# Weight norms moved to TensorE, weight scaling moved to ScalarE, and a first layer that works on column pairs

## The chip, the cores and the metric

The kernel runs on one core of one Trainium2 chip. The metric is device time in microseconds (us) of one execution; the time of before is the median of three runs.

## The reference, cut to what matters

The inputs are float64 or float32 arrays; q, k and v have batch 2, 8 heads, 768 positions, head size 64. The two feed-forward layers have 1536 tokens, model size 512 and hidden size 2048.

```python
q_assign = argmax(q_n . c_n);  k_assign = argmax(k_n . c_n)      # 16 clusters, per head
scores = where(q_assign == k_assign, q @ k.T / 8, -1e9)
x = softmax(scores) @ v                                          # to [1536, 512]
h = x @ w_in;   x = (h * sigmoid(h)) @ w_out                     # "first weights", first layer
h = x @ w2_in;  out = (max(h, 0) + alpha * min(h, 0)) @ w2_out   # second weights, second layer
```

Precision near that of float32 is wanted. So each operand of a matmul is scaled by a power of two and split in a high and a low half in 16 bits, and each product is made of three matmuls (high by high, high by low, low by high).

## The kernel before, in words

**Units.** Attention is cut into 12 query tiles of 128 rows by 8 heads, 96 units. For a unit, `maxima` makes the scores and VectorE takes the row maxima (L514); every second unit `to_rows` (L518) turns the maxima of a pair of units into extra rows of an operand by four small VectorE instructions (L525 to L530), a matmul (L535) and a copy (L537); `weights` makes the scores again, transposed, takes the exponential on ScalarE (L560), makes the high half on ScalarE (L566) and the low half on VectorE (L567); `values` multiplies by v in 20 matmuls (L582 to L592). `x_done` normalises four heads at a time and, after a tile's second half, transposes the tile by a DMA into the operand of the first layer.

**Weights.** Each of the four weight matrices arrives as eight pieces of 1 MB, of float64, so 128 x 1024 numbers of two 32-bit words. `to_f32` (L650) turns a piece into float32: ScalarE converts the low word (L656), the high word is scaled by GpSimd (L664, mode "p") or by ScalarE (L660, mode "a"), and VectorE joins them in two instructions (L667, L670). `sum_sq` (L696) then squares the piece on ScalarE and adds up along the row, a matmul with a matrix of ones (`all_sum`, L222) adds up over the rows, and `pow2_scale` (L171 to L178) makes a power of two of that. `split` (L675) makes the halves: in mode "d" the high one on GpSimd (L677), in mode "a" the same on ScalarE (L682), and in both the low one on VectorE (L678, L683); in mode "b" two instructions are ScalarE's (L687, L688) and one GpSimd's (L689). The strings `SPLIT` and `EXP_ON` (L38, L39) choose the modes piece by piece; their first two entries are the first layer's w_in and w_out. For the first layer's w_in a piece is converted and, one task later, scaled and split; all of w_out is converted first, and its eight splits are run together in `w1_finish` (L789), which the loop calls at step 16 of the first chunk (L1114). GpSimd also makes low halves of k and v (L359, L382).

**First layer.** `layer1` (L899) handles seven chunks of tiles, two of one tile (128 columns) and five of two tiles (256 columns). Each of 16 blocks f of 128 hidden units has 12 matmuls into a PSUM bank (L929), then tanh on ScalarE (L935), a product on VectorE that also frees the bank (L936), the high half on ScalarE (L939) and the low half on VectorE (L940). Then four output blocks take 48 matmuls each (L960) and one ScalarE instruction (L967). The banks come from a pool of two, kind "w".

**Order.** The main loop (L1100 to L1130) runs attention to unit 17, and then gives each chunk 32 steps; after each it advances attention, so that by the end of chunk c the units reach `UNITS_BY_CHUNK[c]` (L24). After a unit, `run_bg` runs as many weight tasks as `W_TASKS` says. The batch-1 keys and values are prepared between units 36 and 56. When the last unit is out, `w2_start` begins the conversion of the second weights, whose buffers lie where attention's keys were; meanwhile the remaining first-layer steps fill TensorE. The build's scheduler then fixes the order of the instructions in each engine's queue; it may place later steps before earlier ones where nothing depends on them. Then `layer2` runs three groups of 512 columns (L1032, L1041 to L1046, L1063).

## Time and profile of before

| what | value |
|---|---|
| median of three runs | 892.24 us (890.08 to 893.33) |
| profiled execution, its own time | 892.16 us |
| its span, first to last instruction | 890.3 us |
| mean granted TensorE clock | 0.986 |
| TensorE matmul busy | 771.0 us (87% of the span) |
| VectorE busy | 622.7 us (70%) |
| ScalarE busy | 481.4 us (54%) |
| GpSimd busy | 151.5 us (17%) |

The profile is of one execution. PE is TensorE's matmuls, PEld its weight loads, DVE is VectorE, ACT is ScalarE, POOL is GpSimd and SP the queue that issues DMAs; L12 is line 12 of the kernel. Ends of matmuls are modelled, so a busy PE is not PE at its peak. Shares over the whole span mix stages with different limits, so the tables below are by stretch, in us from the start of the span. The time outside the span is 892.16 - 890.3 = 1.9 us.

### The profile page before, as it was taken

The page shows a single profiled execution, that of the slowest core. Times are in us where ns is not written, and L with a number is a line of the kernel's source. Part 1 is how long each engine was busy: PE and PEld are TensorE (multiplying, and loading weights), DVE is VectorE, ACT ScalarE, POOL GpSimd, SP SyncE. Part 2 cuts the span into 40 slices and gives each one's busy share as a digit, 9 for nine tenths or more (in the row PEclk, how much of TensorE's full clock was granted, in tenths as well). Part 3 has the DMA queues.
Part 4 walks back from the last instruction along what each step waited for, and adds up shares of the span by engine and source line. Part 5 has one row for each costly group of instructions (what it writes and reads, how often), then busy time and mean ns, then how long its engine had stood idle before and what let it go on. Part 6 is the DMA issues. An engine that isn't in the chain of part 4 may idle for free.

```text
span 890.3 us, 19036 instructions
## 1 busy us (share of the span) xinstructions
PE 771.0 (87%) x8068; PEld 564.9 (63%) x8068; DVE 622.7 (70%) x1379; ACT 481.4 (54%) x817; POOL 151.5 (17%) x142
## 2 busy tenths in 40 slices
PE   2365379889999999999999968969989999999998
PEld 1254268778888788888888856758534444444443
DVE  8999978997987856965876778586896048305700
ACT  7745658846878736755764686787723013102200
POOL 5744200150023210000000003441650000000000
PEclk9999999979999999999999999999999999999999
DMA  8946720322244321120103045444000000000000
GB/s 276 291 114 216 204 64 15 61 59 33 61 83 98 67 62 25 38 48 14 25 14 37 14 147 170 163 149 173 18 1 1 36 13 0 13 25 13 1 23 25
DMA packets 91077, 64.28 MB, mean 72 GB/s; under 512 B 66800, under 2 KB 77040, under 8 KB 90864
## 3 DMA queue, kind: packets, MB, share of 16 engines
q1 hardware_dynamic: 90992, 63.07, 26.6%
q8 instruction: 63, 1.03, 0.5%
q14 instruction: 22, 0.18, 0.1%
HBM read 44.08 MB, written 3.15 MB: 53 GB/s over the span
## 4 chain that ended last, share of the span: by engine, by line
PE 47%; DVE 8%; ACT 4%; DMA 3%; issue 1%; POOL 1%; ACTq 0%; DVEq 0%; POOLq 0%
PE w L1063 9%; PE w L1032 7%; PE w L960 7%; PE w L929 6%; PE m L1063 5%; PE m L1032 4%; PE s L557 2%; PE s L558 2%; DVE arena L1046 2%; DMA arena<-in_moe_w_out_dram 2%; PE s L506 2%; PE s L510 2%; DMA arena<-in_moe_w_in_dram 1%; DVE arena L667 1%; DVE arena L670 1%
## 5 line engine op out<-in xcount | busy, mean ns | idle before, releaser
L929 PE MATMUL w<-arena 128*128 128x256 f16 (+1 forms) x1212 | 129.1, 256 | 6.5 <-DVE arena L936 6.3
L960 PE MATMUL w<-arena 128*128 128x256 f16 (+1 forms) x1200 | 127.3, 259 | 6.5 <-DVE arena L678 4.0
L929 PEld LDWEIGHTS <-arena 128*128 128x128 f16 x1344 | 115.0, 98 | 26.0 <-issue 12.5
L960 PEld LDWEIGHTS <-arena 128*128 128x128 f16 x1344 | 116.3, 100 | 20.0 <-DVE arena L678 4.4
L560 ACT ACTIVATE arena<-s,stat 128x768 f32<-128x768 f32 x96 | 86.2, 898 | 69.9 <-PE s L558 62.8
L514 DVE TENSOR_REDUCE stat<-s 128x1 f32<-128x768 f32 x96 | 91.5, 954 | 40.2 <-PE s L510 39.4
L1032 PEld LDWEIGHTS <-arena 128*128 128x128 f16 x576 | 56.7, 99 | 73.0 <-issue 7.2
L567 DVE TENSOR_TENSOR arena<-arena 128x768 f16<-128x768 f32 x96 | 94.1, 980 | 8.7 <-ACT arena L566 8.3
L1063 PEld LDWEIGHTS <-arena 128*128 128x128 f16 x576 | 56.2, 98 | 68.1
L1032 PE MATMUL w<-arena 128*128 128x512 f16 x384 | 87.8, 385 | 4.0 <-DVE arena L1042 4.0
L664 POOL TENSOR_SCALAR arena<-arena 128x1024 f32<-128x1024 f32 x28 | 40.6, 1454 | 284.5 <-DMA arena<-in_moe_w_in_dram 224.2
L557 PE MATMUL s<-arena 120*128 120x128 f16 x576 | 83.0, 229 | 4.4 <-ACT arena L537 4.3
L1063 PE MATMUL w<-arena 128*128 128x512 f16 x384 | 83.9, 379 | 0.0
L1045 ACT ACTIVATE arena<-arena,stat 128x512 f16<-128x512 f32 x48 | 34.6, 721 | 90.8 <-DVE arena L1042 88.9
L558 PE MATMUL s<-arena 128*128 128x128 f16 x576 | 83.1, 230 | 0.0
L566 ACT ACTIVATE arena<-arena 128x768 f16<-128x768 f32 x96 | 80.3, 836 | 1.1
L588 PE MATMUL x<-arena 128*128 128x65 f16 x576 | 68.7, 198 | 11.2 <-DVE arena L567 11.2
L582 PE MATMUL x<-arena 128*128 128x65 f16 x576 | 74.3, 198 | 4.4 <-ACT arena L566 4.0
L506 PE MATMUL s<-arena 80*128 80x384 f16 x192 | 67.1, 350 | 11.7 <-DMA arena<-arena 6.7
L585 PE MATMUL x<-arena 128*128 128x64 f16 x576 | 74.6, 199 | 0.0
L510 PE MATMUL s<-arena 128*128 128x384 f16 x192 | 67.5, 352 | 0.0
L588 PEld LDWEIGHTS <-arena 128*128 128x128 f16 x576 | 56.4, 102 | 14.5 <-DVE arena L567 12.5
(163 smaller groups left out, 1506.6 us busy)
## 6 DMA issues: line engine op xcount, KB each, us to landing
arena<-in_moe_w_in_dram SPq DMA_DIRECT2D x16, 1024.0 KB, 6.2
arena<-in_moe_w_out_dram SPq DMA_DIRECT2D x16, 1024.0 KB, 4.9
arena<-in_k_dram SPq DMA_DIRECT2D x8, 384.0 KB, 4.4
arena<-in_q_dram SPq DMA_DIRECT2D x6, 512.0 KB, 4.6
arena<-in_v_dram SPq DMA_DIRECT2D x8, 384.0 KB, 6.0
out_dram<-arena SPq DMA_DIRECT2D x12, 256.0 KB, 2.0
arena<-in_moe_alpha_dram SPq DMA_DIRECT2D x1, 1024.0 KB, 4.7
arena<-arena SPq DMA_TRANSPOSE x53, 3.6
```

Of the source, the lines that this page charges most:

```text
L506: nc.tensor.matmul(out=out, lhsT=qt2[0:D + C], rhs=kt2[0:D + C, j * th:(j + 1) * th], start=True, stop=False,)
L510: nc.tensor.matmul(out=out, lhsT=qt1, rhs=kt1[:, j * th:(j + 1) * th], start=False, stop=True,)
L514: nc.vector.tensor_reduce(out=un_cols[:, c:c + 1], in_=sc[:, :, :S // 2], axis=AX.XY, op=ALU.max, negate=True)
L557: nc.tensor.matmul(out=out, lhsT=kt2[0:k, t], rhs=qt2[0:k], start=True, stop=False)
L558: nc.tensor.matmul(out=out, lhsT=kt1[:, t], rhs=qt1, start=False, stop=True)
L560: nc.scalar.activation(out=view(o, F32, 2, S // 2), in_=sc[:, :, :S // 2], func=ACTF.Exp, scale=d[:, pr:pr + 1],)
L567: nc.vector.tensor_tensor(out=pt[:, 1], in0=p, in1=pt[:, 0], op=ALU.subtract)
L588: nc.tensor.matmul(out=out, lhsT=pt[:, T + t], rhs=vt[:, t, 0:D + 1], start=False, stop=False)
L929: nc.tensor.matmul(out=hp, lhsT=wi[:, a, kd, f % 2 * 128:f % 2 * 128 + 128], rhs=mov(bb, kd), start=(i == 0), stop=(i == 3 * KD - 1),)
L960: nc.tensor.matmul(out=acc, lhsT=wo[:, a, f % 2, dt * 128:(dt + 1) * 128], rhs=g[:, f, bb], start=(i == 0), stop=(i == 3 * KF - 1),)
L1032: nc.tensor.matmul(out=hp, lhsT=in_piece(o_a + 24 * KB, f // 2)[:, a, kd, f % 2 * 128:][:, :128], rhs=x[bb][:, kd], start=(i == 0), stop=( ...
L1063: nc.tensor.matmul(out=acc, lhsT=g[:, f, a, t * 128:(t + 1) * 128], rhs=out_piece(o_w, f // 2)[:, bb, f % 2], start=(i == 0), stop=(i == 3 ...
```

## The change

The high word of each piece of the first weights is scaled by ScalarE, not GpSimd; their high halves are made by ScalarE, all sixteen of them (14 were GpSimd's, two of mode "b"). Their sums of squares come from `gram`: eight matmuls of 128 columns multiply the upper 16 bits of a piece's float32 numbers by themselves into one bank, and one VectorE instruction multiplies the diagonal out and adds it up along the row. `layer1` takes two blocks into one bank and does tanh, product, high and low half on both at once; the number of steps stays. `to_rows` has three VectorE instructions, not four, with a constant in another row of the keys' operand, for which `prep_k_a` has two more GpSimd memsets. The chunk targets move. The second weights keep their modes.

```diff
--- before.py
+++ after.py
@@ -21,7 +21,7 @@
 
 
 UNITS_FIRST = 17
-UNITS_BY_CHUNK = (32, 53, 64, 69, 98, 98, 98)
+UNITS_BY_CHUNK = (30, 42, 62, 82, 98, 98, 98)
 W_TASKS = (
     2, 2, 2, 2, 1, 1, 1, 1, 2, 2, 2, 2, 2, 2, 2, 2,
     1, 1, 1, 1, 2, 2, 3, 2, 1, 1, 1, 1, 1, 1, 1, 1, 1, 1, 1, 1, 2, 2, 2, 2,
@@ -35,8 +35,8 @@
 
 K_SCALE_ON = ("aaaa", "pppa")
 V_SCALE_ON = ("papa", "appp")
-SPLIT = ("dddddddd", "dddbdddb", "dbdbdbdb", "dccdcbbc")
-EXP_ON = ("pppppppp", "pppppppp", "appppapp", "papapppp")
+SPLIT = ("aaaaaaaa", "aaaaaaaa", "dbdbdbdb", "dccdcbbc")
+EXP_ON = ("aaaaaaaa", "aaaaaaaa", "appppapp", "papapppp")
 
 
 
@@ -119,7 +119,7 @@
     o_g = region(16 * KB)
     o_x2 = region(24 * KB)
     o_xt = region(12 * KB)
-    o_tmp = region(3 * KB)
+    o_tmp = region(4 * KB)
     o_a = region(0)
     o_kt1 = region(12 * KB)
     o_kt2 = region(12 * KB)
@@ -137,6 +137,7 @@
     o_id = region(256)
     o_ml = region(256)
     o_sel = region(288)
+    o_junk = region(256)
     o_one = region(1024)
     total = pos[0]
     arena = arena_p.tile([128, total // 4], F32, name="arena")
@@ -347,6 +348,8 @@
         for i in range(2):
             r = MROW + 2 * (2 * pr + i)
             nc.gpsimd.memset(w2[:, i * T:(i + 1) * T, r:r + 2], MASK)
+            r = FROW + 2 * pr + i
+            nc.gpsimd.memset(w2[:, i * T:(i + 1) * T, r:r + 1], -MASK)
         if b == 0 and pr == 0:
             s = kv_state.pop("s")
             nc.scalar.activation(out=w1[:, :, D:2 * D], in_=kr, func=ACTF.Copy, scale=s)
@@ -403,9 +406,9 @@
                     stop=(t == T - 1),
                 )
         hi, lo = sv[:, 0, 4 * w:4 * w + 4], sv[:, 1, 4 * w:4 * w + 4]
-        nc.scalar.activation(out=hi, in_=ps, func=ACTF.Copy, scale=2.0 ** -5)
+        nc.scalar.activation(out=hi, in_=ps, func=ACTF.Copy, scale=1.0 / MASK)
         nc.vector.scalar_tensor_tensor(
-            out=lo, in0=ps, scalar=2.0 ** -5, in1=hi, op0=ALU.mult, op1=ALU.subtract
+            out=lo, in0=ps, scalar=1.0 / MASK, in1=hi, op0=ALU.mult, op1=ALU.subtract
         )
 
     def v_scales(b):
@@ -521,14 +524,15 @@
         n, h = divmod(u, H)
         pr = h // 2
         nm = un_cols[:, 2 * (u // 2 % 3):2 * (u // 2 % 3) + 2]
-        c = scr(2)
-        nc.vector.tensor_scalar(c, nm, 2.0 ** 29, 1.0 / MASK, op0=ALU.min, op1=ALU.mult)
         r = MROW + 4 * pr
         parts = ml[:, r:r + 4].rearrange("p (a b) -> p a b", b=2)
-        nc.vector.tensor_copy(out=parts[:, :, 0], in_=c)
-        nc.vector.tensor_tensor(out=parts[:, :, 1], in0=c, in1=parts[:, :, 0], op=ALU.subtract)
+        nc.vector.tensor_scalar(parts[:, :, 0], nm, 1.0 / MASK, None, op0=ALU.mult)
+        nc.vector.scalar_tensor_tensor(
+            out=parts[:, :, 1], in0=nm, scalar=1.0 / MASK, in1=parts[:, :, 0],
+            op0=ALU.mult, op1=ALU.subtract,
+        )
         nc.vector.tensor_scalar(
-            ml[:, FROW + 2 * pr:FROW + 2 * pr + 2], nm, 2.0 ** 29, 2.0 ** 5,
+            ml[:, FROW + 2 * pr:FROW + 2 * pr + 2], nm, 2.0 ** 29, MASK,
             op0=ALU.is_ge, op1=ALU.mult,
         )
         ps = psum("m", 128)
@@ -695,6 +699,18 @@
     def sum_sq(t, junk, ss):
         nc.scalar.activation(out=junk, in_=t, func=ACTF.Square, accum_out=ss)
 
+    def gram(tb, ss):
+
+
+        ps = psum("w", 128)
+        for i in range(PC // 128):
+            c = tb[:, i * 128:(i + 1) * 128]
+            nc.tensor.matmul(out=ps, lhsT=c, rhs=c, start=(i == 0), stop=(i == PC // 128 - 1))
+        nc.vector.scalar_tensor_tensor(
+            out=view(o_junk, BF16, 128), in0=ps, scalar=1.02, in1=ident, op0=ALU.mult,
+            op1=ALU.mult, accum_out=ss,
+        )
+
     def in_tasks(w, raws, o_dst, kind, modes, mp):
 
         m = Weight()
@@ -712,7 +728,10 @@
         def conv(j):
             t, junk = (raw(j)[:, :, i].bitcast(F32) for i in (1, 0))
             to_f32(raw(j), t, mp[j])
-            sum_sq(t, junk, ss[:, j:j + 1])
+            if w2:
+                sum_sq(t, junk, ss[:, j:j + 1])
+            else:
+                gram(view(raws[j % len(raws)], BF16, PC, 4)[:, :, 3], ss[:, j:j + 1])
 
         def scale(j):
             if not w2:
@@ -757,7 +776,10 @@
                     assert ("k", 0, o // 6) in did
             t = view(o_ts[j], F32, PC)
             to_f32(raw(j), t, mp[j])
-            sum_sq(t, raw(j)[:, :, 0].bitcast(F32), ss[:, j:j + 1])
+            if w2:
+                sum_sq(t, raw(j)[:, :, 0].bitcast(F32), ss[:, j:j + 1])
+            else:
+                gram(view(o_ts[j], BF16, PC, 2)[:, :, 1], ss[:, j:j + 1])
             load(j + len(raws))
 
         def scale():
@@ -914,32 +936,34 @@
         first = t0 % T == 0
         if c and first:
             nc.vector.tensor_scalar(dh, w1["in"].inv, x_inv[b], 0.5, op0=ALU.mult, op1=ALU.mult)
-        for f in range(KF):
-            j = f // 2
+        for j in range(NPC):
             wi = in_piece(o_w, j)
-            if c == 0 and f % 2 == 0:
+            if c == 0:
                 nc.vector.tensor_scalar(
                     dh[:, j:j + 1], w1["in"].inv[:, j:j + 1], x_inv[b], 0.5,
                     op0=ALU.mult, op1=ALU.mult,
                 )
-            hp = psum("l", n)
-            i = 0
-            for kd in range(KD):
-                for a, bb in ((0, 0), (0, 1), (1, 0)):
-                    nc.tensor.matmul(
-                        out=hp, lhsT=wi[:, a, kd, f % 2 * 128:f % 2 * 128 + 128], rhs=mov(bb, kd),
-                        start=(i == 0), stop=(i == 3 * KD - 1),
-                    )
-                    i += 1
-            th = view(o_tmp + KB * ring("t1", 3), F32, n)
-            nc.scalar.activation(out=th, in_=hp, func=ACTF.Tanh, scale=dh[:, f // 2:f // 2 + 1])
+            hp = psum("l", 2, n)
+            for r in range(2):
+                i = 0
+                for kd in range(KD):
+                    for a, bb in ((0, 0), (0, 1), (1, 0)):
+                        nc.tensor.matmul(
+                            out=hp[:, r], lhsT=wi[:, a, kd, r * 128:r * 128 + 128], rhs=mov(bb, kd),
+                            start=(i == 0), stop=(i == 3 * KD - 1),
+                        )
+                        i += 1
+                if r == 0:
+                    yield
+            th = view(o_tmp + 2 * KB * ring("t1", 2), F32, 2, n)
+            nc.scalar.activation(out=th, in_=hp, func=ACTF.Tanh, scale=dh[:, j:j + 1])
             nc.vector.scalar_tensor_tensor(
                 out=th, in0=th, scalar=1.0, in1=hp, op0=ALU.add, op1=ALU.mult
             )
-            nc.scalar.activation(out=g[:, f, 0], in_=th, func=ACTF.Copy, scale=2.0 ** -16)
+            hi, lo = g[:, 2 * j:2 * j + 2, 0], g[:, 2 * j:2 * j + 2, 1]
+            nc.scalar.activation(out=hi, in_=th, func=ACTF.Copy, scale=2.0 ** -16)
             nc.vector.scalar_tensor_tensor(
-                out=g[:, f, 1], in0=th, scalar=2.0 ** -16, in1=g[:, f, 0],
-                op0=ALU.mult, op1=ALU.subtract,
+                out=lo, in0=th, scalar=2.0 ** -16, in1=hi, op0=ALU.mult, op1=ALU.subtract,
             )
             yield
         g1_done.add(c)
```

## Rows read from the trace of the kernel before

**Rows 1.** Stretches: busy us (x) of PE, PEld, DVE, ACT, POOL; clock; DMA.

```profile
40.00:133.00 93.00, 50.62 (x562) 40.57 (x563) 86.60 (x162) 51.69 (x72) 33.05 (x21) 0.98 0.56 157
...
176.00:194.00 18.00, 13.81 (x164) 12.15 (x162) 18.00 (x15) 7.85 (x11) 14.32 (x12) 0.72 0.13 33
...
194.00:320.00 126.00, 116.68 (x1889) 103.62 (x1887) 101.91 (x304) 92.85 (x178) 19.30 (x20) 1.00 0.38 76
...
320.00:525.00 205.00, 203.48 (x2752) 179.55 (x2751) 145.92 (x397) 125.23 (x219) 1.32 (x1) 1.00 0.15 28
...
525.00:665.00 140.00, 113.12 (x889) 84.04 (x887) 111.67 (x164) 95.54 (x159) 56.96 (x32) 0.96 0.37 125
```

**Rows 2.** Timeline, 91 to 94 us: start, us, engine, instruction.

```profile
91.18 1.13 POOL L664 TENSOR_SCALAR arena<-arena 128x1024 f32<-128x1024 f32 x1 [1.13 <-DMA arena<-in_moe_w_out_dram]
...
91.43 1.95 DVE L667 SCALAR_TENSOR_TENSOR arena<-arena 128x1024 int32<-128x1024 int32 x1
```

**Rows 3.** DVE groups, 40 to 133 us; last, L667 over the span, min/median/max.

```profile
L667 DVE SCALAR_TENSOR_TENSOR arena<-arena 128x1024 int32<-128x1024 int32 x14 | 22.5, 1610 | 2.6 <-POOL arena L664 1.5 <-ACT arena L537 1.1
...
L670 DVE SCALAR_TENSOR_TENSOR arena<-arena 128x1024 int32<-128x1024 int32 x14 | 18.9, 1348 | 0.0
...
L667 DVE SCALAR_TENSOR_TENSOR arena<-arena x32: 1207/1226/2608, 14.7 to 627.2; 128x1024 int32<-128x1024 int32 x32
```

**Rows 4.** POOL groups, 40 to 133 us.

```profile
L664 POOL TENSOR_SCALAR arena<-arena 128x1024 f32<-128x1024 f32 x13 | 18.5, 1433 | 29.1 <-DMA arena<-in_moe_w_out_dram 27.3 <-ACT arena L696 1.8
...
L677 POOL TENSOR_SCALAR arena<-arena,stat 128x1024 f16<-128x1024 f32 x6 | 12.1, 2022 | 13.4 <-DVE stat L178 10.9 <-DVE stat L175 2.4
```

**Rows 5.** Two PE matmuls at 107 us; PE group of fp32 matmuls, whole span.

```profile
107.29 0.31 PE L557 MATMUL s<-arena 120*128 120x128 f16 x1
...
107.40 0.31 PE L558 MATMUL s<-arena 128*128 128x128 f16 x1
...
L222 PE MATMUL m<-arena 128*128 128x128 f32 x4 | 1.3, 409 | 4.7 <-DVE arena L407 4.7
```

**Rows 6.** ACT groups of the span, 1024 wide.

```profile
L696 ACT ACTIVATE arena<-arena 128x1024 f32<-128x1024 f32 x32 | 36.9, 1152 | 30.5 <-DVE arena L670 27.8 <-DVE stat L175 2.7
...
L660 ACT ACTIVATE arena<-arena 128x1024 f32<-128x1024 f32 x4 | 4.5, 1116 | 0.0
...
L696 ACT ACTIVATION_READ_ACCUMULATOR arena<-arena 128x1 f32 x32 | 6.2, 195 | 0.0
```

**Rows 7.** DVE and POOL groups, 173 to 194 us; then DVE timeline there.

```profile
L678 DVE SCALAR_TENSOR_TENSOR arena<-arena,stat 128x1024 f16<-128x1024 f32 x6 | 12.9, 2188 | 0.0
...
L677 POOL TENSOR_SCALAR arena<-arena,stat 128x1024 f16<-128x1024 f32 x6 | 9.3, 1571 | 58.2 <-DVE stat L950 58.2
...
178.91 1.27 DVE L678 SCALAR_TENSOR_TENSOR arena<-arena,stat 128x1024 f16<-128x1024 f32 x1
```

**Rows 8.** DVE groups: three of 320 to 525 us, two of 665 to 890.

```profile
L936 DVE SCALAR_TENSOR_TENSOR arena<-arena,w 128x256 f32<-128x256 f32 x42 | 17.4, 417 | 1.7 <-ACT arena L935 1.4
...
L940 DVE SCALAR_TENSOR_TENSOR arena<-arena 128x256 f16<-128x256 f32 x42 | 17.5, 420 | 5.2 <-ACT arena L939 5.2
...
L529 DVE TENSOR_TENSOR arena<-stat,arena 128x2 f16<-128x2 f32 x22 | 3.5, 158 | 0.2
...
L1042 DVE SCALAR_TENSOR_TENSOR arena<-w,arena 128x512 f32<-128x512 f32 x26 | 17.8, 686 | 0.2
...
L1046 DVE SCALAR_TENSOR_TENSOR arena<-arena,stat 128x512 f16<-128x512 f32 x39 | 29.1, 746 | 4.8 <-ACT arena L1045 4.6
```

**Rows 9.** PE group, 495 to 525 us; SP timeline there.

```profile
L929 PE MATMUL w<-arena 128*128 128x256 f16 x120 | 14.8, 273 | 0.0
...
525.41 21.36 SPq L645 DMA_DIRECT2D arena<-in_moe_w_in_dram  x3
```

**Rows 10.** Waits over the span: us in total, times, longest.

```profile
DVE stat L171 <- PE m L222: 7.4, 8, 2.3
...
PE w L929 <- DVE arena L936: 6.3, 9, 2.3
```

## The prediction

> **What bounds the kernel now.** I read the stretches first [rows 1], then the groups of the stretches where TensorE waits. In each stretch, compare TensorE's and VectorE's busy time with its length. From 320 to 525 us TensorE is busy 203.5 of 205.0 us: only less matmul work ahead of something counts there. After 665 us it is full with the second layer, which the change leaves alone. The loss lies in three places. In the ramp (40 to 133 us) TensorE is busy 50.6 of 93 us and VectorE 86.6: VectorE bounds it, converting the first weights. At 176 to 194 us VectorE is busy for all of 18.0 us while TensorE waits 4.2 us and its mean granted clock is 0.72; `w1_finish` makes its eight splits there. From 525 to 665 us the second weights are converted while the rest of the first layer fills TensorE (113 of 140 us); VectorE is busy 111.7 us and GpSimd 57.0.
>
> The second reading is what makes VectorE so busy. L667 takes 1.226 us in its median [rows 3]. The one that started just after GpSimd began a scaling took 1.95 us [rows 2], and the ramp's mean is 1.610 [rows 3]. So a VectorE instruction with two inputs in SBUF is held while GpSimd works. The Trainium skill, "SBUF — State Buffer", section "Who interferes with whom", says that such an instruction contends with a GpSimd one that reads SBUF, and that the one issued second blocks until the other is done. By that rule the stretching goes with the GpSimd work that the change takes away; the rows agree, 0.7 us beyond the median on that instruction.
>
> **The change part by part.** The sum stands against the profiled execution's 892.16 us, 0.08 below the median of 892.24.
>
> *Ramp.* Both GpSimd groups go, 18.5 + 12.1 = 30.6 of its 33.05 us there [rows 1, 4]. L667 and L670, of the same form, lose their stretching: 14 x (1.610 - 1.226) = 5.4 and 14 x (1.348 - 1.226) = 1.7 us [rows 3]; smaller groups are held too and I put 3 us on them, an estimate from those two (their excess is 0.25 per instruction; a dozen more are held). VectorE's 1.5 us of waiting for L664 goes [rows 3]. One instruction fewer in five `to_rows` is 5 x 0.16 = 0.8 us [rows 8]. Together -12.4. Against it stand 14 of the 16 new diagonal sums, on 128 columns from PSUM. The trace has no such instruction: below, a 256-wide product from PSUM takes 0.417 us; above, the 512-wide 0.686 [rows 8] plus an accumulator read as ScalarE has, 0.195 [rows 6]. The narrower size is the nearer one, so 0.42: +5.9. Net -6.5; with VectorE busy 93% of the stretch I count **-6**.
>
> ScalarE takes over 14 scalings at 1.116 and 6 high halves at about 1.15 and gives up 14 squares at 1.152 + 0.195 [rows 6]: 15.6 + 6.9 - 18.9 = +3.6, so 55 of 93 us [rows 1], hidden by VectorE's 80. If VectorE became so fast that ScalarE led, those 3.6 us would be the cost. TensorE gets 14 x 8 matmuls of 128 columns, 0.11 apart in the ramp [rows 5]: 12.3 us in 42 idle ones. They read every second or fourth 16-bit number, which no row shows. Bounds: 0.11 as for packed ones, and 0.41 of a float32 matmul of that size [rows 5], 46 us in all, 4 more than is idle. I take 0.11: the column count and the element size are the same. The Trainium skill, "SBUF — State Buffer", section "Specifications (TRN2)", gives 16-byte lines that want two hits each; by that both strides (4 and 8 bytes) run free and the sum keeps 0.11. No run here shows it. Bounds of the ramp: -14 (all stretching gone, sums at 0.2 us) to +10 (the dear matmuls).
>
> *`w1_finish`.* Six L678 took 2.188 us each, 13.1; eight at 1.27 are 10.2 [rows 7], the two more because mode "b" had its low half on GpSimd. Behind these pieces TensorE's L960 waits: 4.2 us idle, and a clock of 0.72 [rows 1], one of its two levels, 1.2 GHz, for over half of the stretch. ScalarE's eight high halves (9.2 us) fit: it is busy 7.9 of 18. What is late next is VectorE itself, 10.2 us beside two attention units. **-5**, bounds -9 (all idle time and clock loss) to 0.
>
> *133 to 320 us, the rest.* A merged pair of blocks saves VectorE 2 x 0.417 - 0.686 = 0.15 in the product and 2 x 0.420 - 0.746 = 0.09 in the low half [rows 8]; three chunks have 24 pairs: 5.8 us. `to_rows` saves 20 x 0.16 = 3.2. TensorE is idle 9.3 of the long stretch's 126 us, VectorE 24 [rows 1], so a third of 9.0 is worth time: **-3**, bounds -9 to 0. For 320 to 525 us, with the pairs of two more chunks, I count nothing: TensorE covers it, and were it less full, 16 x 0.24 + 22 x 0.16 = 7.4 us of VectorE would show.
>
> *Targets.* Attention's end decides when the second weights can be loaded, at 525.4 us [rows 9]. Before that TensorE ran 120 matmuls of the sixth chunk's first layer, 14.8 us [rows 9], though nothing needs them before 525 and 27 us are idle later [rows 1]. Chunk 4 spanned 29 units, heavy on VectorE; now 16, and chunks 2 and 3 take 20 each instead of 11 and 5. Each is then led by TensorE, with little gap for the scheduler to fill from the next chunk. So 14.8 us move behind attention's end, and VectorE's five pairs, 5 x (0.686 + 0.746) = 7.2 us at 80% load, come back as 5.7. **-9**, bounds -15 to +3 (moved units find their keys late).
>
> *525 to 665 us.* Two chunks' pairs save 16 x 0.24 = 3.8 us of VectorE, half of it on the path: **-2**, bounds -4 to 0. The sixteen more memsets and the fewer DMA waits of GpSimd cost nothing; nobody waits for GpSimd in the ramp but VectorE. No DMA is moved; a w_out buffer is free one ScalarE instruction earlier.
>
> Sum: -6 - 5 - 3 - 9 - 2 = -25, so **867 us**.
>
> **The rivals.** (A) *Only ramp and finish count.* The scheduler again lifts first-layer work ahead of attention's end, and the middle stays full: -11 to -14, 880. For it: the order in the queues isn't the program's, as the 120 matmuls show. (B) *VectorE's relief works in full*: the lower ends but for half the targets, -14 - 9 - 9 - 7 - 3 = -42, 850. For it: VectorE leads ramp and finish at 93 and 100%. Against it: no resource here gives back every saved microsecond.
>
> (C) *Slower: VectorE stands at the head of its queue for the new sums.* A sum waits for its eight matmuls, which stand in TensorE's queue behind attention matmuls that wait themselves; all conversion behind it on VectorE stands too, and units wait for that. The existing norm has such waits of 0.9 us mean, 2.3 longest [rows 10]. At 0.9, 16 cost 15 us (882); at 2.3, 37: **904**. It decides from 1.6 us per sum (25 / 16). Against it: only 8 such waits fell on the "m" sums in the whole span.
>
> (D) *No gain*: the ramp is held by loads, since GpSimd waited 27.3 us there for pieces of w_out [rows 4], and the targets give as much as they take: 890. Against it: VectorE, not GpSimd, is the busy one.
>
> (E) *Larger instructions make bubbles.* A bank waits for tanh and product of two blocks, and TensorE's 6.3 us of waiting for L936 [rows 10] doubles; with the same again for the banks of the last chunks, +10: 877. The Trainium skill, "Perfetto Trace Analysis", section "Optimizing Scalar/DVE Operations", advises the opposite of pairing where Vector and Scalar aren't saturated but cause bubbles: break instructions up. By that rule it is E; the trace bears it out little, since in the middle TensorE is full.
>
> **How the numbers follow.** Chances: forecast 0.45, A 0.26, B 0.10, C 0.09, D 0.06, E 0.04. The likeliest gives 867. The range 850 to 886 holds forecast, A, B and E and the milder C; beyond it lie the 904 of C and D. A difference of 0.5%, 4.5 us, is about what a measurement of this kernel can tell from none. Faster by more: 0.45 + 0.26 + 0.10 + 0.04 = 0.85. D's 890 lies within: 0.06. Slower: C's 0.09.
>
> **What would show it.** Ramp: L667 and L670 near 1.22 us, GpSimd under 10 us from 40 us on, the first L929 some 6 us earlier; wrong if VectorE idles on the new sums (C) or they take 0.9 us. Finish: eight low halves within 13 us and a clock above 0.72. Targets: the second weights' loads some 23 us earlier than 525.4, and few first-layer matmuls of the sixth chunk before them; if these are again over a hundred, A holds. The prediction is wrong if the loads come no earlier, or if the stretch between them and the second layer grows by over 8 us.

## The result, and the profile after

The changed kernel takes 877.23 us in the median (875.5 to 878.42), against 892.52 of the kernel before (now of four runs): a ratio of 0.9832, with a 95% interval from 0.9805 to 0.9858. Forecast were 867 (850 to 886): the sign and the range held, the gain of 15 was forecast as 25. The profiled execution took 876.54 us, its span is 874.6, and the mean granted clock 0.963.

First the stretches of the changed kernel, in the columns of [rows 1].

```profile
40.00:123.50 83.50, 53.32 (x622) 44.17 (x623) 75.66 (x185) 55.44 (x62) 0.00 (x0) 0.71 0.63 178
123.50:187.00 63.50, 56.38 (x973) 51.15 (x973) 50.99 (x118) 45.75 (x73) 1.65 (x10) 0.97 0.25 50
187.00:320.00 133.00, 128.36 (x1972) 115.46 (x1970) 101.00 (x262) 89.07 (x145) 19.41 (x23) 1.00 0.34 64
320.00:508.50 188.50, 182.94 (x2563) 160.39 (x2560) 137.08 (x324) 113.88 (x167) 1.59 (x1) 0.99 0.18 33
508.50:665.00 156.50, 133.09 (x1011) 95.74 (x1009) 123.80 (x174) 103.07 (x154) 57.12 (x32) 0.97 0.32 111
```

GpSimd is silent in the ramp, as meant. (The clock column's 0.71 there, for 0.98 in [rows 1], is not a fall of the clock; the last section shows why.) But from 320 us on, where TensorE had been busy for 203.5 of 205.0 us [rows 1], it now idles 188.5 - 182.9 = 5.6 us. The stage bounds, read from the first and last matmul of each kind, tell more:

| point | before, us (units whose maxima are done) | after |
|---|---|---|
| first matmul of the first layer | 133.7 (13) | 123.5 (12; the 13th ends 0.3 later) |
| end of the first chunk | 209.7 (32) | 186.6 (27) |
| end of the fourth chunk | 413.0 (70) | 381.3 (64) |
| start of the fifth chunk | 415.0 (71) | 401.4 (70) |
| attention's end: its last score matmul | 524.8 | 508.6 |
| from there to the end of the span | 365.5 | 366.0 |

Three things are to be seen. The first layer runs ahead of attention: at these chunks' ends fewer units are done than before, so the 23 us won at the end of the first chunk are not 23 us of progress. Nor are the 10.2 us at its first matmul: before, that followed the `values` matmuls of ten units, now it follows those of eight. The maxima of the 13th unit ended at 128.0 us before and end at 123.8 now, 4.1 us earlier. And the whole gain is there at attention's end (16.2 us); nothing is won or lost behind it. The row for that end, in the kernel before and in the changed one (minimum, median, maximum in ns; first and last start in us):

```profile
L558 PE MATMUL s<-arena x576: 218/220/315, 53.8 to 524.8; 128*128 128x128 f16 x192
```

```profile
L562 PE MATMUL s<-arena x576: 219/219/314, 50.2 to 508.6; 128*128 128x128 f16 x192
```

Next, VectorE's groups of the changed kernel, 40 to 123.5 us: the two conversions, and the new sum with its accumulator read.

```profile
L674 DVE SCALAR_TENSOR_TENSOR arena<-arena 128x1024 int32<-128x1024 int32 x14 | 18.3, 1309 | 0.0
L671 DVE SCALAR_TENSOR_TENSOR arena<-arena 128x1024 int32<-128x1024 int32 x13 | 15.9, 1220 | 4.1 <-ACT arena L664 4.1
...
L709 DVE SCALAR_TENSOR_TENSOR arena<-w,arena 128x128 bf16<-128x128 f32 x14 | 4.0, 283 | 0.6 <-PE w L708 0.5
...
L709 DVE DVE_READ_ACCUMULATOR arena<-w,arena 128x1 f32 x14 | 1.1, 81 | 0.0
```

L671, the L667 of [rows 3], fell from a mean of 1.610 to 1.220 us, near its old median of 1.226. L674, the old L670, stayed at 1.309 (1.348 before) though GpSimd is silent, so most of its excess had another cause. A sum costs 0.283 + 0.081 = 0.36 us. It waits for TensorE 0.5 us in all; the long wait of the new work stands on the other side, in TensorE's queue, as its waits over the span and its group for 40 to 123.5 us show:

```profile
PE w L708 <- DVE arena L674: 13.9, 7, 3.4
PE s L509 <- DMA arena<-arena: 12.8, 6, 3.4
...
PE m L539 <- DVE arena L530: 8.3, 3, 5.1
...
PE w L951 <- DVE arena L960: 2.9, 4, 1.3
```

```profile
L708 PE MATMUL w<-arena 128*128 128x128 bf16 x112 | 14.0, 289 | 11.9 <-DVE arena L674 11.9
```

The norm matmuls (L708) stand at the head of TensorE's queue until VectorE has converted the piece, 13.9 us in seven waits, with attention's matmuls behind them. The wait for paired blocks (L951 for L960) is shorter than its like of [rows 10], 2.9 for 6.3 us.

### The profile page after: what moved, and what is told of

Read it like the earlier page. It is cut to its first block, busy times and chain, and to the rows that moved or that the text cites. A ratio compares the mean times of both kernels' runs of the same rounds, so it can differ in the third digit from the quotient of the medians.

```text
span 874.6 us, 19047 instructions
## 1 busy us (share of the span) xinstructions
PE 772.2 (88%) x8196; PEld 570.1 (65%) x8196; DVE 590.0 (67%) x1253; ACT 476.0 (54%) x701; POOL 100.3 (11%) x126
## 4 chain that ended last, share of the span: by engine, by line
PE 61%; DVE 16%; DMA 8%; ACT 6%; issue 2%; POOL 2%; DVEq 0%; POOLq 0%; SPq 0%; ACTq 0%
PE w L1087 9%; PE w L984 9%; PE w L951 8%; PE w L1056 8%; PE m L1087 5%; PE m L1056 4%; DMA arena<-arena 4%; DMA arena<-in_moe_w_in_dram 3%; PE s L509 3%; PE s L561 3%; PE s L562 3%; PE s L513 3%; DVE arena L674 2%; DVE arena L671 2%; DVE arena L687 2%
## 5 line engine op out<-in xcount | busy, mean ns | idle before, releaser
L951 PE MATMUL w<-arena 128*128 128x256 f16 (+1 forms) x1200 | 126.2, 257 | 4.6 <-DVE arena L960 2.9
L951 PEld LDWEIGHTS <-arena 128*128 128x128 f16 x1344 | 115.3, 99 | 18.3 <-issue 3.6
L1056 PEld LDWEIGHTS <-arena 128*128 128x128 f16 x576 | 56.7, 99 | 76.3 <-issue 10.6
L561 PE MATMUL s<-arena 120*128 120x128 f16 x576 | 80.6, 225 | 3.8 <-ACT arena L541 2.8
L1065 DVE TENSOR_SCALAR arena<-w,stat 128x512 f32<-128x512 f32 x32 | 23.9, 748 | 87.2 <-PE w L1056 86.7
L562 PE MATMUL s<-arena 128*128 128x128 f16 x576 | 80.5, 225 | 0.0
```

Of the source, the lines that this page charges most:

```text
L561: nc.tensor.matmul(out=out, lhsT=kt2[0:k, t], rhs=qt2[0:k], start=True, stop=False)
L562: nc.tensor.matmul(out=out, lhsT=kt1[:, t], rhs=qt1, start=False, stop=True)
L951: nc.tensor.matmul(out=hp[:, r], lhsT=wi[:, a, kd, r * 128:r * 128 + 128], rhs=mov(bb, kd), start=(i == 0), stop=(i == 3 * KD - 1),)
L1056: nc.tensor.matmul(out=hp, lhsT=in_piece(o_a + 24 * KB, f // 2)[:, a, kd, f % 2 * 128:][:, :128], rhs=x[bb][:, kd], start=(i == 0), stop=( ...
```

## The experiments

All times are medians beside runs of the kernel before (892.35 to 893.27 us in the four sets). "Bare" is the longest stretch between the first chunk and attention's end in which TensorE has no first-layer matmul for its waits, the last units left out ("none": none over 4 us). "Behind" is the span less the last score's start. The last three columns are of the profiled execution, which is up to 2.6 us off the median (run 12's, 873.65 us, is the slowest of its five).

| run | kernel | us | ratio, 95% | bare, us | attention's end | behind |
|---|---|---|---|---|---|---|
| 1 | change, old modes | 899.36 | 1.0055 to 1.0106 | 31.6 | 530.2 | 366.8 |
| 2 | change, old targets | 877.71 | 0.9812 to 0.9850 | 20.1 | 509.8 | 366.1 |
| 3 | change, single blocks | 873.42 | 0.9748 to 0.9807 | none | 503.7 | 367.0 |
| 4 | change, norms on ScalarE | 873.14 | 0.9761 to 0.9819 | 9.0 | 503.3 | 366.5 |
| 5 | change, bank ring turned | 877.74 | 0.9811 to 0.9850 | 20.0 | 508.5 | 366.3 |
| 6 | change, norms later | 873.86 | 0.9764 to 0.9808 | 14.2 | 504.0 | 366.2 |
| 7 | before, new modes | 881.75 | 0.9855 to 0.9896 | 4.8 | 514.0 | 364.3 |
| 8 | run 7, new rows and targets | 872.49 | 0.9749 to 0.9791 | none | 505.4 | 364.2 |
| 9 | run 7, new rows | 878.48 | 0.9819 to 0.9858 | none | 512.1 | 364.2 |
| 10 | change, norms later, single blocks | 870.73 | 0.9731 to 0.9768 | none | 501.6 | 364.6 |
| 11 | change, old rows | 888.81 | 0.9940 to 0.9986 | 40.4 | 519.7 | 366.4 |
| 12 | change, first chunk after 14 units | 871.06 | 0.9729 to 0.9775 | 7.7 | 501.0 | 370.6 |

**Runs 1 to 4: each part undone alone.** Theory: each part is worth about its term of the forecast.

```diff
-SPLIT = ("aaaaaaaa", "aaaaaaaa", "dbdbdbdb", "dccdcbbc")
-EXP_ON = ("aaaaaaaa", "aaaaaaaa", "appppapp", "papapppp")
+SPLIT = ("dddddddd", "dddbdddb", "dbdbdbdb", "dccdcbbc")
+EXP_ON = ("pppppppp", "pppppppp", "appppapp", "papapppp")
```

> The changed kernel with the two strings of modes as before: high words and high halves of the first weights again on GpSimd, the norms still on TensorE. Theory (the gain of the ramp and of w1_finish is VectorE's freedom from GpSimd): first first-layer matmul at about 132 us instead of 123.5, chunk 0 ends 15 us later than 186.6, and the time is 887 to 892. Rival (the gain is from targets and pairs): 877 to 880, and the ramp no more than 3 us longer.

```diff
-UNITS_BY_CHUNK = (30, 42, 62, 82, 98, 98, 98)
+UNITS_BY_CHUNK = (32, 53, 64, 69, 98, 98, 98)
```

> The changed kernel with the chunk targets as before. Theory (the new targets keep 48 matmuls, 5.2 us, of the sixth chunk behind attention, but leave a stretch of 20 us, 381 to 401, without first-layer work and 3.6 us idle there): 875 to 880, over 100 of the sixth chunk's matmuls again before the last scores, no bare stretch. Rival (the targets are worth the 9 us I forecast): 884 to 888.

```diff
-        for j in range(NPC):
+        for f in range(KF):
...
-            hp = psum("l", 2, n)
+            hp = psum("l", n)
```

> The changed kernel with the first layer's elementwise work block by block again. Theory (VectorE and ScalarE have time to spare where TensorE is full; only the stretch of the second weights feels it): 878 to 882, VectorE 13 us busier in all, ScalarE 20. Rival 1 (pairs lengthen the hold of a bank and cost time): 870 to 875. Rival 2 (the pairs are the main gain): 885 to 890.

```diff
-            if w2:
-                sum_sq(t, junk, ss[:, j:j + 1])
-            else:
-                gram(view(raws[j % len(raws)], BF16, PC, 4)[:, :, 3], ss[:, j:j + 1])
+            sum_sq(t, junk, ss[:, j:j + 1])
...
-            if w2:
-                sum_sq(t, raw(j)[:, :, 0].bitcast(F32), ss[:, j:j + 1])
-            else:
-                gram(view(o_ts[j], BF16, PC, 2)[:, :, 1], ss[:, j:j + 1])
+            sum_sq(t, raw(j)[:, :, 0].bitcast(F32), ss[:, j:j + 1])
```

> The changed kernel with the sums of squares on ScalarE again, scaling and high halves still ScalarE's. Theory (the norms are hidden either way: TensorE stood 13.9 us before them in the ramp, but had the time; ScalarE has 28 of 83 us free): 875 to 881, ramp within 3 us of 123.5. Rival (ScalarE would become the bound of the ramp, so that the norms had to leave it): 885 to 890, ScalarE over 90% busy from 40 us to the first layer.

Without the new modes the rest makes the kernel slower than before: the modes are worth 899.4 - 877.2 = 22 us within the change. The targets are worth 0.5 us, no more than the spread of the runs. Pairs and norms stand against it: undone alone, each leaves the kernel some 4 us faster. The interval of the change (0.9805 to 0.9858) touches those of runs 3 and 4 at the edge, so the sign is likelier than the size.

The early start of the first layer needs modes and norms together: it is at 134.8 us in run 1 and in run 4, as late as before, and for run 4 within 3 us of 123.5 was expected. Run 4, with the norms on ScalarE, is the faster one all the same: 16 units are done at its start, and its attention ends 5.3 us ahead of the change's. The start says little of the time.

Why the targets do nothing can be read off the order in which TensorE works: with old and new ones the first 4793 of its 8196 matmuls, up to 404.6 us, start in the same order, and in both traces the first four chunks end after 27, 41, 52 and 64 units. So run 2 met the time of its theory, but neither of its signs (over a hundred matmuls, no bare stretch). The forecast's sign for this was the sixth chunk's matmuls ahead of attention's end; the changed kernel, 478 to 508.5 us, has 72 of them, for 120 before [rows 9]:

```profile
L951 PE MATMUL w<-arena 128*128 128x256 f16 x72 | 8.9, 272 | 0.0
```

That number doesn't change in run 2 either: most of it comes from the pairs (108 in run 3). Only with single blocks do the new targets move some, 120 in run 9 and 108 in run 8.

**Run 5: the pairs and the ring of banks.** Run 3's second layer starts 1.7 us later than the change's but is 5.6 us shorter, from start to end (259.3 for 264.9), though its code is the same. The PE groups of 609 to 665 us, first of the changed kernel, then of run 3, show where: in its first matmuls' wait for VectorE.

```profile
L1056 PE MATMUL w<-arena 128*128 128x512 f16 x120 | 28.8, 391 | 7.2 <-DVE arena L1066 7.2
```

```profile
L1054 PE MATMUL w<-arena 128*128 128x512 f16 x132 | 31.5, 394 | 2.8 <-DVE arena L1064 2.8
```

Theory: the pairs only shift the turn of the three banks. The edit skips one turn.

```diff
     def layer2(j):
+        if j == 0:
+            ring("l", 3)
         x = x2_parts(j)
```

> The changed kernel, but one turn of the three-bank ring is skipped ahead of the second layer, so that its first blocks take the banks in the order w, w, m, as in the kernel before and in the run with single blocks, not m, w, w. Nothing ahead of the second layer is touched. Theory 'the pairs cost by the ring': with single blocks the stretch from the second layer's start to the end was 259.3 us long, with pairs 264.9, though the second layer itself is the same code; the pairs only halve the number of banks taken before and so shift the ring. Then the 5 us come back: 872 to 873 us, and the waits of the second layer's first matmuls for VectorE fall from 7.2 to about 3 us. Rival 'the pairs cost ahead of it' (banks held longer, second layer late for another reason): 877, waits as before.

877.74 us, the waits 6.3 us for 7.2: the theory finds no support. (The first blocks now take the banks in the order w, m, w; run 3's take w, w, m, so its order was not quite restored.) What run 3 gains in the second layer it had lost ahead of it; the column "behind" says so, 367.0 for 366.0. This is so in all the kernels: from its first matmul to the end the second layer lasts 258.7 to 260.7 us in the six with single blocks and 264.4 to 266.5 in the eight with pairs, yet but for run 12 "behind" differs by less than 3 us. The pairs' loss lies ahead of attention's end.

**Run 6: where the norms stand in the queue.**

```diff
             if w2:
                 sum_sq(t, junk, ss[:, j:j + 1])
-            else:
-                gram(view(raws[j % len(raws)], BF16, PC, 4)[:, :, 3], ss[:, j:j + 1])
+            elif j:
+                norm(j - 1)
...
```

(`norm(j)` is the old call of `gram`; the last piece's stands ahead of its scale, and w_out is treated alike.)

> The changed kernel, but each piece's sum of squares on TensorE is issued one piece later, after the next piece's conversion. The work is the same, 128 matmuls; what goes is TensorE's waiting at the head of its queue for the conversion (13.9 us in 7 waits). Theory 'head of the queue': most of the 4 us that the norms cost come back, 873 to 874, and those waits fall under 4 us. Theory 'occupancy': the 16.2 us of matmuls displace attention work whatever their place, 876 to 878. A later sum can also delay the scale of a w_in piece and so the first layer's start: up to 5 us slower than 877.

873.86, with all 128 matmuls still there. TensorE's waits of the run for that conversion:

```profile
PE w L708 <- DVE arena L674: 9.4, 5, 3.8
```

They fell by 4.5 us, less than expected (under 4 us were to be left), and the time by 3.4. So most of the 4 us hangs on the place of the norms in the queue, not on the matmuls' own time. The edit reorders other work too (the bare stretch is 14.2 us long, not 20.1), and this run doesn't part the two.

**Runs 7 to 9: modes, rows and targets without pairs and norms.** Run 7 is the kernel before with the lines that run 1 takes away; run 8 is the change with the edits of runs 3 and 4; run 9 is run 8 with that of run 2.

> The kernel before with nothing but the new modes: scaling and high halves of the first weights on ScalarE. Theory 'the modes carry the gain and the rest gives some back' (pairs -4, norms -4, targets 0): 868 to 872 us, faster than the full change. Theory 'the modes need the norms off ScalarE' (ScalarE would be busy some 74 of 93 us in the ramp and lead there): 877 to 885.

> The changed kernel with single blocks and with the sums of squares on ScalarE again: what stays is modes, three instead of four instructions for the rows, and the targets. If the two costs seen alone (4.1 and 3.8 us against 877.2) add up: 869 us. If both are one cost (the first layer starts later without the norms on TensorE, and the pairs' cost is lost in the same wait): 872 to 873.

> The run with modes and shorter row preparation (872.5 us), but with the old chunk targets. It stands 9.3 us below the modes alone (881.8); this run divides that between the two parts. Theory 'the rows': the shorter chain of to_rows is worth it, 872 to 873 here. Theory 'the targets' (they count only where blocks are single, since there 108 first-layer matmuls of the sixth chunk stand before attention's end and with the old targets 120): 880 to 882. Halfway would be 877.

The modes alone bring 10.6 us, and no earlier start: the first layer begins at 133.6 us. The time lies where the second theory had it, and the ramp fits that theory: ScalarE, still with the norms, is busy 77 of the 93.6 us from 40 us to there, and VectorE waits 12.0 us for its scaling, for 4.1 in the change. Yet run 4 has the norms there too, with a wait of 12.7, and is faster than the change. VectorE's group of run 7 from 40 to 133.5 us:

```profile
L667 DVE SCALAR_TENSOR_TENSOR arena<-arena 128x1024 int32<-128x1024 int32 x14 | 17.5, 1251 | 12.0 <-ACT arena L660 12.0
```

The rows bring 881.75 - 878.48 = 3.3 more (the two intervals touch); the targets, worth nothing within the change, 878.48 - 872.49 = 6.0 here, and here the order of the matmuls parts early (after 1168 of 8068, at 159 us). Pairs and norms together cost 877.2 - 872.5 = 4.7. The parts don't add: norms cost 0.9 us with single blocks (run 3 less run 8) and 4.1 with pairs, pairs 0.6 with the norms on ScalarE (run 4 less run 8) and 3.8 with them on TensorE. With four runs each and a spread of up to 5 us, this last difference, of pairs and norms, is not clear of the noise; those of the modes (22 and 10.6 us) and of the targets (0.5 and 6.0) are.

**Run 10: both repairs.** The edits of runs 3 and 6.

> The changed kernel with both repairs: sums of squares one piece later (alone 873.9) and single blocks (alone 873.4). If the two add up: 870. If what decides is attention's end, with some 366 us behind it in every run so far: the idle time saved in the middle (about 4 us) is spent on 36 more matmuls of the sixth chunk ahead of that end (36 x 0.109 = 3.9 us), so 873 to 874.

870.73 us, the lowest median of all, though not clear of run 12, and faster than both kernels: its interval ends at 0.9768, the change's begins at 0.9805. The two repairs add up (-3.8 and -3.4; together -6.5).

**Run 11: the old rows.** Within the change, `to_rows` and what belongs to it as before.

```diff
-        nc.vector.tensor_scalar(parts[:, :, 0], nm, 1.0 / MASK, None, op0=ALU.mult)
-        nc.vector.scalar_tensor_tensor(
-            out=parts[:, :, 1], in0=nm, scalar=1.0 / MASK, in1=parts[:, :, 0],
-            op0=ALU.mult, op1=ALU.subtract,
-        )
+        nc.vector.tensor_scalar(c, nm, 2.0 ** 29, 1.0 / MASK, op0=ALU.min, op1=ALU.mult)
...
+        nc.vector.tensor_copy(out=parts[:, :, 0], in_=c)
+        nc.vector.tensor_tensor(out=parts[:, :, 1], in0=c, in1=parts[:, :, 0], op=ALU.subtract)
```

> The changed kernel with the old row preparation (four dependent VectorE instructions on two columns, not three, and no extra memsets). The forecast counted the shorter chain at 0.16 us per pair of units on VectorE, some 2 us in all: 878 to 880 here. Theory 'TensorE waits at the head of its queue for the chain': the stretch up to attention's end grows by 5 to 9 us and the matmul of the rows waits longer than 8.3 us in total: 883 to 886.

888.81: the rows are worth 11.6 us within the change, more than either theory gave. The stretch without first-layer work, 20.1 us in the change, is 40.4 here. Its row for that stretch, and TensorE's longest waits in it, in run 11:

```profile
367.50:407.90 40.40, 29.85 (x440) 23.93 (x438) 29.77 (x83) 23.03 (x32) 0.00 (x0) 0.87 0.26 47
```

```profile
PE m L536 <- DVE arena L530: 6.5, 2, 3.2
PE x L589 <- DVE arena L568: 1.6, 3, 1.1
PE s L558 <- ACT arena L538: 1.1, 3, 0.5
```

The same row of the changed kernel, with its longest wait, and the row of run 3, where the fifth chunk follows at once:

```profile
381.30:401.40 20.10, 16.54 (x272) 13.67 (x270) 15.86 (x42) 13.22 (x18) 0.00 (x0) 0.92 0.30 54
```

```profile
PE m L539 <- DVE arena L530: 2.2, 1, 2.2
```

```profile
376.00:395.00 19.00, 19.00 (x265) 16.65 (x263) 12.49 (x34) 10.95 (x16) 0.00 (x0) 1.00 0.26 57
```

In run 11's stretch no engine is full: TensorE and VectorE are each busy 30 of 40 us, ScalarE 23. Attention alone is a chain from engine to engine, and the matmul of the rows (L536), which waits for the four small VectorE instructions, has the longest of its waits. Over the span it waits 14.3 us for them, for 8.3 in the change. In run 3's stretch, with first-layer work at hand, TensorE has no idle time. Idle time plus lost clock is 10.55 + 0.13 x 40.4 = 15.8 us in run 11 and 3.56 + 0.08 x 20.1 = 5.2 in the change: 10.6 of the 11.6 us (an estimate; with the clock counted over the busy time alone it is 9.5).

The instruction itself can't be worth that much: at 0.16 us for each of 48 pairs of units it is 7.7 us if every one were on the path. The edit also lets the first layer run further ahead (the first chunk ends after 23 units, for 27, and the fourth after 59, for 64), and how much of the 11.6 us is the chain and how much this order isn't shown.

**Run 12: the stretch shortened by itself.** No instruction changes.

```diff
-UNITS_FIRST = 17
+UNITS_FIRST = 14
```

> The changed kernel with the first chunk opened after 14 units, not 17; no instruction is added or taken away. In TensorE's queue this leaves fewer attention matmuls alone between the first pair of the fifth chunk and the rest of it (some 6 us of work where the changed kernel has 14). Theory 'bare attention': the time lost in the middle is that of stretches in which attention stands alone and TensorE has no first-layer work to fill its waits (20 us long, from 381 to 401 us, in the changed kernel; 40 us in the run with the old row preparation). Then the bare stretch falls to 8 to 14 us, the idle time between the end of the first chunk and attention's end from 10.2 to about 7, and the time to 873 to 875. Rival 'the pairs cost elsewhere': 877, with the same idle time.

```profile
386.30:394.00 7.70, 5.75 (x100) 4.41 (x98) 7.09 (x19) 5.44 (x8) 0.00 (x0) 1.00 0.74 138
```

The bare stretch of run 12 is 7.7 us long and loses 2.0; idle time from the first chunk's end to attention's end fell from 10.2 to 6.5 us, and the time to 871.06, below what was expected. The two rows from which that idle time is read, of the change and of run 12:

```profile
186.60:508.60 322.00, 311.80 (x4541) 276.35 (x4539) 238.13 (x587) 203.19 (x313) 21.00 (x24) 0.99 0.25 46
```

```profile
188.90:501.00 312.10, 305.60 (x4487) 271.72 (x4485) 230.78 (x569) 198.61 (x307) 20.66 (x24) 1.00 0.24 46
```

So the stretch costs time, and the same instructions can do without most of it. The kernels that have pairs and the new modes fall in line with it: 871.1 us at a bare stretch of 7.7 us, 873.1 at 9.0, 873.9 at 14.2, 877.2 to 877.7 at 20, 888.8 at 40.4, though each differs from the others in more than the stretch. That all 6.2 us are its doing isn't shown: in the profiled execution attention's end came 7.6 us earlier, and 3.7 of these are that idle time; the first chunk's end, too, had 29 units done at 188.9 us, for 27 at 186.6.

## Why the prediction was right in sign and short in size

By stage, forecast and measured are: up to the first layer's first matmul -6 and -10.2 us; from there to attention's end -17 and -6.0 (391.1 us, now 385.1); behind it -2 and +0.5.

- **Ramp (-6).** Right in sign: VectorE was busy 75.7 us, where 80 were forecast. But the 10.2 us aren't its worth, since the first layer now starts after fewer units; the 13th unit's maxima came 4.1 us earlier. Nor does VectorE's freedom from GpSimd shorten the ramp alone: in run 7 VectorE waits for ScalarE instead. L667's stretching went as said, L670's 1.7 us for the most part not (1.309 us without GpSimd). The Trainium skill's rule on a VectorE instruction with two SBUF inputs beside GpSimd ("SBUF — State Buffer", section "Who interferes with whom") agrees: 1.610 with GpSimd at work, 1.220 without, while ScalarE was busy 55 of 83 us. The sum cost 0.36 us where 0.42 was taken, a norm matmul 14.0 / 112 = 0.125 where 0.11 was. The term's bounds, -14 and +10, don't follow from what is written beside them: -12.4 and 14 sums at 0.2 us make -9.6, and matmuls 4 us over the idle time don't make +10. What was missed is the other end of it: TensorE waits 13.9 us at the head of its queue.
- **`w1_finish` (-5).** Right in its working: eight low halves of 1.27 us, where six took 2.19 each [rows 7], within 13 us, and the clock is 1.00 where it was 0.72. VectorE is as full as it was and TensorE idles 4.0 us for 4.2, so what changed most there is the clock. The VectorE group of 155 to 172 us, and the row of 155 to 173:

```profile
L687 DVE SCALAR_TENSOR_TENSOR arena<-arena,stat 128x1024 f16<-128x1024 f32 x8 | 9.9, 1273 | 0.0
```

```profile
155.00:173.00 18.00, 14.04 (x253) 12.08 (x251) 17.44 (x32) 14.51 (x16) 1.65 (x10) 1.00 0.35 86
```

  Runs 7 and 1 measure what the modes bring in ramp and finish together, with very different partners: 10.6 us and 22. In run 7 most of it is won here: from the first layer's first matmul to the first chunk's end it takes 66.9 us, for 76.0 before, though with 17 units for 19.
- **Targets (-9).** The step that failed. "14.8 us move behind attention's end" took the targets for an order; run 2 gives 0.5 us. The trace of the kernel before could have warned: its first five chunks end with 32, 48, 55, 70 and 89 units done, where its targets say 32, 53, 64, 69 and 98, so that the fifth spanned 18 units and not the 29 of the forecast. The second weights' loads came 16.2 us earlier (509.2 us for 525.4), as attention's end did, where 23 were said. Without the targets' term the sum is -16, 876 us; measured were 877.2. That is no proof of the other terms, since further errors cancel within it:
- **133 to 525 us (-3, and nothing from 320 on).** "TensorE covers it" was true of the kernel before and no longer of the changed one, in which the pairs and the place of the norms let the first layer run ahead (the fourth chunk ends with 64 units done, in runs 3, 4 and 6, which undo or mend them, with 70, 68 and 67), so that it was used up while attention went on alone. The new modes and rows work against that: without them that number is 60 (run 1) and 59 (run 11), and the stretch is longer (31.6 and 40.4 us). In the stretch the wait for the rows' chain is the longest. The forecast priced the chain at 0.16 us an instruction; the edit to it was worth 3.3 us in run 9 and 11.6 in run 11.
- **525 to 665 us (-2).** Nothing: 365.5 and 366.0 us from attention's end on. In twelve of the fourteen kernels, the two of the change among them, it is 364.2 to 366.8, run 3 has 367.0, though 72 to 120 of the sixth chunk's 192 first-layer matmuls were done before. So that stretch isn't set by how much of the first layer is left. That the second weights' conversion sets it was only argued. Run 12's 370.6 goes with a lower clock, 0.92 from 501 to 606.7 us, for 0.97 in the same stage of the change; which brings the other isn't shown.
- **The rivals.** (C) fell: VectorE waits 0.5 us in the ramp for its new sums. (A) gave 880 by the scheduler lifting first-layer work forward while the middle stays full: the first happened, though with 72, not "over a hundred", matmuls, and the second did not. (B) and (D), 850 and 890, fell with the time. (E) gave 877, the time measured, for a cause that isn't there: the waits for the bank fell. The rule beside it, of the Trainium skill, "Perfetto Trace Analysis", section "Optimizing Scalar/DVE Operations", is that where VectorE and ScalarE aren't saturated but cause bubbles on other engines, smaller instructions may let work be done sooner. Run 3 bears out its advice (3.8 us) but not its reason: the loss shows not as waits at the bank but in the order of the work, which the pairs change.

What stays open: why the build's order follows the targets in one kernel and not in the other, and how far each experiment's own reordering is in its number.

## What to carry to other kernels

Where filler work hides the waits of a dependent chain, ask of every part that speeds the filler up how long it will last: once it is used up, the chain's own waits are on the path, and a part that seemed worth 2 us measured 3.3 in one kernel and 11.6 in another. A part's worth is then a matter of its partners; undo each within the change and try each alone before adding terms up. And read from the order in the trace, not from the program, whether a target moves work at all.

## What the runs showed of the hardware that was not expected

The norm matmuls read every second 16-bit number (the eight pieces of w_out, a stride of 4 bytes) or every fourth (the eight of w_in, 8 bytes), for both operands. At the clock's upper level, where packed score matmuls (L562) start 0.06 us apart, those of w_out start 0.057 apart: their stride is free. Those of w_in start 0.118 apart, half the rate. The rows, PE timeline of the changed kernel; a merged row ends with its last matmul:

```profile
50.81 0.22 PE L562 MATMUL s<-arena 128*128 128x128 f16 x1
50.87 1.11 PE L708 MATMUL w<-arena 128*128 128x128 bf16 x8
...
110.50 0.22 PE L562 MATMUL s<-arena 128*128 128x128 f16 x1
110.56 0.62 PE L708 MATMUL w<-arena 128*128 128x128 bf16 x8
```

At the lower level w_out's start 0.107 apart, as packed ones do, and w_in's still 0.118, in every kernel here that has the norms on TensorE. So the 0.11 of the forecast, the packed price at the lower level, was near, for w_in by luck, and its bound of 0.41 far off. The rule of the Trainium skill, "SBUF — State Buffer", section "Specifications (TRN2)", by which both strides run free, agrees for 4 bytes and not for 8; the measurement decides. Which of the two operands costs the time isn't shown.

The clock falls in the middle of the kernel too, after a stretch with idle time. In the changed kernel's PE timeline, score matmuls start 0.06 us apart at the head of the bare stretch and 0.11 apart near its end, so at half the rate; the clock's two levels are 1.2 and 2.4 GHz.

```profile
381.44 0.22 PE L561 MATMUL s<-arena 120*128 120x128 f16 x1
381.50 0.22 PE L562 MATMUL s<-arena 128*128 128x128 f16 x1
...
399.75 0.31 PE L562 MATMUL s<-arena 128*128 128x128 f16 x1
399.86 0.31 PE L561 MATMUL s<-arena 120*128 120x128 f16 x1
```

By that spacing the ramp of the kernel before, too, ran at the lower level at 107 us, 0.11 apart [rows 5], where its clock column says 0.98 [rows 1]. Of its 99 spacings between neighbouring score matmuls from 40 to 123 us 87 are at least 0.10 us, in the changed kernel 61 of 110. So the spacing is the safer reading. A run's mean clock says little: executions of the kernel before with a mean granted clock of 0.943 and of 0.988 took 890.9 and 891.5 us.
